# First attention pass with keys stationary, and a list scheduler that prices TensorE's tiling modes

## The chip, the cores and the metric

The kernel runs on one core of one Trainium2 chip. The time is device microseconds of one execution, from launch to the last store; runs of the kernel before took 632.1, 632.15 and 632.55 us (median 632.15). Profiles come from one execution that the hardware profiler recorded.

## What is computed

Two batches of eight heads, 1152 keys, head size 64. Queries are averaged in pairs, so each head has 576 of them. Then two dense layers follow on the 1152 rows that the attention gives.

```python
q_pool = q.reshape(B, H, S // 2, 2, D).mean(axis=3)
scores = scale * np.matmul(q_pool, k.transpose(0, 1, 3, 2))
scores = scores - np.max(scores, axis=-1, keepdims=True)
attn = np.exp(scores)
attn = attn / (np.sum(attn, axis=-1, keepdims=True) + 1e-09)
x = np.matmul(attn, v)                       # -> 1152 x 512
h = x @ w_in                                 # 512 -> 2048
g = np.maximum(h, 0.0) + np.log1p(np.exp(-np.abs(h)))
x = g @ w_out                                # 2048 -> 512
h = np.maximum(np.maximum(x @ w1, x @ w2), x @ w3)
out = h @ w_out2                             # 512 -> 768 -> 512
```

A common shift in place of each row's maximum gives the same softmax, as long as no exponential overflows and no sum gets too small; the kernel judges that at the end and would run a slow exact program if it failed.

## The kernel before

The heads are worked in eight pairs; the two heads of a pair lie on partitions 0 to 63 and 64 to 127, so that two matmuls with 64 contraction rows run side by side. Three arrangements of TensorE occur. In *row* matmuls (64*128 in the profile) the array is split by rows, one half for each head: the scores (`st`, tile by tile transposed, and `s`). In *column* matmuls (128*64) it is split by columns: values (`x`) and sums (`l`). *Whole-array* matmuls (128*128) are transposes of queries and keys (`tq`, `tk`), the spreading of the maximum (`tm`), the tail scores and all of the dense layers.

For each pair there are two passes. The first pass (`first_pass`, `scores`, `part_max`) finds a bound on the scores: a rough product of high halves, `s`, with queries stationary (128 at a time) and keys streaming in 384 columns; each result fills a PSUM bank, and VectorE reduces it to a maximum (L916). Four tiles of 128 queries make twelve row pairs. The last 64 queries of both heads stand together in a block-diagonal tile `qd` and make three whole-array matmuls (L904). `whole_max`, `spread` (L941) and `keep_shift` turn the maxima into a shift, one after six of nine row sets and one after all. The second pass (`one_unit`, `turned`, L956) computes the scores again, transposed and with three terms, in units of half a pair's queries (288 columns; three smaller units for pair 0): for each of nine key tiles a *block* `st` of six row matmuls into two banks, two exponentials on ScalarE (L966) that free the banks, an add into `acc` (L975, on GpSimd, one in each odd unit on VectorE), and for each three key tiles a group `x` (L983). `l` (L997) sums up.

PSUM has eight banks: two for `x`, six that `tq`, `tk`, `s`, `st`, `tm`, `l` and early weight conversion share. A bank is free again when the engine that reads it has finished.

The order of all this is made by `Order`, a list scheduler: every piece has an engine, a cost and a place; in a simulated timeline the piece with the lowest place among those that can start goes next. The first pass of pair n+1 is mixed into the second pass of pair n in this way. Weights of the first dense layer are converted with the lowest priority. Engines keep the order so found; each waits on semaphores.

Of the kernel before, what the change touches and what calls it, by code (L numbers as in the profile page):

```python
# [33 lines left out]
AK = {"load": -419.68, "load1": -714.981, "q1": -406.536, "k1": 649.535, "v0": 1846.393, "p1": 0.482, "p2": 18.929, "kl": 220.139, "c0": -292.838, "v": 170.415, "q": -14.042, "k": -7.013, "pass": 14.039, "gap": 4.467, "values": 59.704, "sum": 64.591}  # L34
WINDOW = 48.719
NPT = 20
ON_DVE = ((), (7,))
# [4 lines left out]
PAIR = 0.22  # L42
# [11 lines left out]
class Order:  # L54
# [3 lines left out]

    AFTER = {"PE": 0.30, "ACT": 0.22, "DVE": 0.20, "POOL": 0.22, "SP": 2.6, "AQ": 2.6}

    def __init__(self, **pools):
        self.work = []
        self.wrote = {}
        self.read = {}
        self.pools = pools
        self.got = {}
        self.ahead = {}

# [73 lines left out]
def kernel(  # L142
# [601 lines left out]
    else:  # L744
        order = Order(s=6)
        TRIO = 0.42
# [6 lines left out]
        NX = 2 * NT + 1  # L753
        ROWS = (0, 1, 2, NT, NT + 1, NT + 2, 3, NT + 3, 2 * NT)
        STEPS = ((0, 6), (6, NX))
        FIRST_ROWS = (0, NT, 1, 2, NT + 1, NT + 2, 3, NT + 3, 2 * NT)
        FIRST_STEPS = ((0, 2), (2, 6), (6, NX))
        KT = NJ // NB

# [3 lines left out]
        qds = []  # L763
        for n in range(2):
            qd = st.tile([P, P], F32R, tag=f"qd{n}", name=f"qd_{n}")
            nc.gpsimd.memset(qd.bitcast(F32), 0.0)
            qds.append(qd)
# [91 lines left out]
        def tail_q(pr, i, n):  # L859
            o = (NT - q_parts(pr)[1][0]) * QB  # L860
            nc.scalar.mul(qds[pr % 2][halves(i), halves(i)], tiles[n][halves(i), o : o + D], Q_SCALE)

# [36 lines left out]
        def scores(pr, t, g, *ns):  # L899
            qh, kh = tiles["qh", pr], tiles["kh", pr]  # L900
            cols = slice(g * BK, (g + 1) * BK)
# [10 lines left out]
        def part_max(pr, x, g, n):  # L912
            if ("nh", pr) not in tiles:
                tiles["nh", pr] = sm.tile([P, NX, NB], F32, tag=f"nh{pr % 2}", name=f"nh_{pr}")
            at = rows(pr).index(x)
            nc.vector.tensor_reduce(  # L916
                out=tiles["nh", pr][:, at, g : g + 1], in_=tiles[n][:, :BK], axis=AX.X, op=ALU.max, negate=True
            )
# [4 lines left out]
        def rows(pr):  # L923
            return ROWS if pr else FIRST_ROWS

        def rows_of(pr, step):
            return (STEPS if pr else FIRST_STEPS)[step]

        def whole_max(pr, step):
            if ("nm", pr) not in tiles:  # L930
                tiles["nm", pr] = sm.tile([P, 3], F32, tag=f"nm{pr % 2}", name=f"nm_{pr}")
                tiles["shift", pr] = sm.tile([P, 3], F32, tag=f"shift{pr % 2}", name=f"shift_{pr}")
            z = rows_of(pr, step)[1]
            nc.vector.tensor_reduce(
                out=tiles["nm", pr][:, step : step + 1], in_=tiles["nh", pr][:, :z], axis=AX.XY, op=ALU.min
            )
# [113 lines left out]
        def name_of(n):  # L1050
            return f"b{n[1]}"
# [6 lines left out]
        def prepare_first():  # L1058
# [4 lines left out]
            for g, (t0, t1) in enumerate(q_parts(0)):  # L1063
# [4 lines left out]
                if g:  # L1068
                    for i in range(2):
                        order.add("ACT", 0.16, p + 1, tail_q, 0, i, n, reads=(name_of(n),), writes=(f"qd0{i}",))  # L1070
# [8 lines left out]
        def prepare(pr):  # L1079
# [6 lines left out]
            for g in range(2):  # L1086
# [3 lines left out]
                if g:  # L1090
                    for i in range(2):
                        order.add("ACT", 0.16, p, tail_q, pr, i, n, reads=(name_of(n),), writes=(f"qd{y}{i}",))
# [7 lines left out]
        def first_pass(pr):  # L1100
            y = pr % 2
            gap = AK["gap"] if pr else 2.0
            k = 0
            for step, (a, z) in enumerate(STEPS if pr else FIRST_STEPS):
# [3 lines left out]
                some = rows(pr)[a:z]  # L1108
                for t in sorted({NT if x == 2 * NT else x % NT for x in some}):
                    xs = (2 * NT,) if t == NT else (t, NT + t)  # L1110
                    for g in range(NB):
                        p = at + gap * k
                        k += len(xs) / NB
                        ns = [next_bank() for _ in xs]
                        order.add("PE", PAIR if len(xs) == 2 else 0.18, p, scores, pr, t, g, *ns,
                                  reads=[f"kh{y}{g}", f"tq{y}", f"tk{y}"] + ([f"qd{y}0", f"qd{y}1"] if t == NT else [f"qh{y}{int(t >= (3 if pr else 1))}"]),
                                  writes=[name_of(n) for n in ns], take=tuple(ns))
                        for x, n in zip(xs, ns):
                            order.add("DVE", 0.49, p, part_max, pr, x, g, n, reads=(name_of(n),), writes=(f"nh{y}_{x}{g}",), free=n)
                p = at + gap * k  # L1120
                n = next_bank()
                order.add("DVE", 0.16, p - 2, whole_max, pr, step, reads=[f"nh{y}_{x}{g}" for x in some for g in range(NB)],
# [4 lines left out]
        def one_unit(u):  # L1127
# [3 lines left out]
            for j in range(NJ):  # L1131
# [3 lines left out]
                order.add("PE", TRIO * max(part, 0.8), p, turned, u, j, *ns,  # L1135
# [9 lines left out]
            for js in VALUES:  # L1145
                p = at + gap * js[-1] + AK["values"] * part
                order.add("PE", 0.48 * len(js) * part + 0.15, p, values, u, js,
                          reads=[f"p{(u * NJ + j) % NPT}" for j in js] + [f"v{y}"], writes=(f"x{u % 2}",))
            n, p = next_bank(), at + gap * NJ + AK["sum"] * part
            order.add("PE", (0.54 + 0.48 * len(DIRECT)) * part, p, sum_up, u, n,  # L1150
# [403 lines left out]
```

## Time and profile before

| | us |
|---|---|
| median of three runs | 632.15 |
| the profiled execution, by its own time | 632.11 |
| its span, first to last instruction | 630.3 |
| TensorE busy in the span | 607.8 |
| VectorE, ScalarE, GpSimd busy | 411.2, 355.6, 356.3 |
| last attention matmul ends and the first dense layer begins | 265.42 |

The attention fills the span up to 265.42 us, the dense layers the rest. In the profile a matmul in 32-bit floats (`x`, `l`, `tm`) shows as two records. A matmul's length in the timeline holds the way through the array, which the next one overlaps; how long a stretch of TensorE's work took is therefore read from one row's start to the next row's start. "Idle before" in brackets is the time in which nothing was in the array, and who ended it.

### The profile page before, as it was taken

The numbers are of one execution on the slowest core, as the hardware profiler recorded it, in microseconds if no ns is written. First come the engines' busy times: TensorE is split into PE (matmuls) and PEld (weight loads), VectorE is DVE, ScalarE is ACT, GpSimd is POOL, SyncE is SP. The second block draws the span as 40 slices with busy tenths as digits, with TensorE's granted clock in tenths as the row PEclk, the third lists the DMA queues.
The fourth block names the chain that finished last, engine by engine and source line by source line (L and its number), as shares of the span: only waits on it lengthen the run. The fifth ranks groups of instructions, "written<-read, shape, count | busy, mean of one in ns | idle before, by whom it ended". The sixth has DMA issues, their size and how long they took to land.

```text
span 630.3 us, 10804 instructions
## 1 busy us (share of the span) xinstructions
PE 607.8 (96%) x3992; PEld 510.6 (81%) x3992; DVE 411.2 (65%) x797; ACT 355.6 (56%) x833; POOL 356.3 (57%) x304
## 2 busy tenths in 40 slices
PE   6999999999999999999999999999999999999995
PEld 4766665666666565689999999999999999999994
DVE  6575757575758898688988897987879831121221
ACT  2557676766676777887767666775754312012101
POOL 1457676767678678399888787797865200000000
PEclk9999999999999999999999999999999999999999
DMA  6412131404051323123434243322323201000001
GB/s 156 145 39 77 38 92 23 109 6 116 33 143 35 106 68 101 35 68 105 124 108 125 82 128 101 108 93 68 100 80 123 68 1 51 0 2 35 17 1 56
DMA packets 53296, 46.68 MB, mean 74 GB/s; under 512 B 20592, under 2 KB 47216, under 8 KB 53232
## 3 DMA queue, kind: packets, MB, share of 16 engines
q1 hardware_dynamic: 51408, 45.29, 24.4%
q10 hardware_dynamic: 1824, 0.59, 0.4%
q8 instruction: 33, 0.54, 0.4%
q14 instruction: 31, 0.25, 0.1%
HBM read 43.52 MB, written 2.36 MB: 73 GB/s over the span
## 4 chain that ended last, share of the span: by engine, by line
PE 81%; ACT 6%; POOL 6%; issue 2%; DVE 2%; DMA 1%; ACTq 0%; SPq 0%; POOLq 0%
PE bank_h_m L1220 18%; PE bank_y L1220 15%; PE bank_h L1220 13%; PE x L983 10%; PE st L956 10%; PE bank_o L1220 6%; ACT p L966 4%; PE s L908 3%; POOL acc L975 2%; PE l L997 2%; PE tk L878 1%; POOL d L1275 1%; DVE nh L916 1%; PE tq L844 1%; PE s L904 1%
## 5 line engine op out<-in xcount | busy, mean ns | idle before, releaser
L966 ACT ACTIVATE p<-st,shift 128x288 f32<-128x288 f32 (+2 forms) x306 | 126.8, 487 | 65.8 <-PE st L956 58.9
L975 POOL TENSOR_TENSOR acc<-acc,p 128x576 f32<-128x576 f32 (+2 forms) x88 | 117.2, 1332 | 28.2 <-ACT p L966 24.2
L916 DVE TENSOR_REDUCE nh<-s 128x1 f32<-128x384 f32 x216 | 108.7, 550 | 32.1 <-PE s L908 27.3
L1220 PE MATMUL bank_h_m<-x,wh 128*128 128x384 f32 x432 | 114.1, 337 | 0.0
L1220 PE MATMUL bank_h<-x,wh 128*128 128x384 f32 x384 | 106.0, 338 | 0.7 <-DVE gl L1299 0.7
L241 POOL TENSOR_SCALAR size<-size 128x512 f32<-128x512 f32 x56 | 84.1, 1505 | 18.7 <-ACT size L236 18.7
L983 PE MATMUL x<-p,v 128*64 128x288 f32 (+2 forms) x612 | 81.5, 403 | 0.0
L1220 PEld LDWEIGHTS bank_h_m<-x,wh 128*128 128x128 f32 x432 | 78.8, 188 | 0.7
L956 PE MATMUL st<-qh,kh 64*128 64x288 f32 (+2 forms) x306 | 69.9, 358 | 6.3 <-ACT p L966 5.2
L1220 PE MATMUL bank_h_m<-x,wl 128*128 128x384 f32 x216 | 72.9, 337 | 0.0
L1220 PEld LDWEIGHTS bank_h<-x,wh 128*128 128x128 f32 x384 | 70.3, 188 | 1.4 <-DVE gl L1299 1.0
L956 PEld LDWEIGHTS st<-qh,kh 64*128 64x128 f32 x306 | 38.8, 192 | 39.4 <-ACT p L966 18.8
L1220 PE MATMUL bank_y<-gh,wh 128*128 128x384 f32 x192 | 65.2, 340 | 1.4 <-DVE gl L1299 1.4
L1220 PE MATMUL bank_y<-gl,wh 128*128 128x384 f32 x192 | 65.0, 339 | 0.0
L1220 PE MATMUL bank_y<-gh,wl 128*128 128x384 f32 x192 | 65.0, 339 | 0.0
L1220 PE MATMUL bank_h<-x,wl 128*128 128x384 f32 x192 | 64.9, 338 | 0.0
L1275 POOL TENSOR_TENSOR d<-e,d 128x384 f32<-128x384 f32 x48 | 49.0, 1020 | 25.7 <-DVE d L1268 23.9
L983 PEld LDWEIGHTS x<-p,v 128*64 128x64 f32 x612 | 39.7, 138 | 26.7 <-issue 8.2
L956 PE MATMUL st<-ql,kh 64*128 64x288 f32 (+2 forms) x306 | 56.7, 312 | 0.0
L956 PE MATMUL st<-qh,kl 64*128 64x288 f32 (+2 forms) x306 | 52.4, 297 | 0.0
L1284 POOL TENSOR_TENSOR d<-u,d 128x384 f32<-128x384 f32 x48 | 49.0, 1021 | 3.7
L1337 DVE TENSOR_TENSOR mg<-bank_h_m,mg 128x384 f32<-128x384 f32 x18 | 10.0, 555 | 61.5 <-PE bank_h_m L1220 61.5
(223 smaller groups left out, 1153.4 us busy)
## 6 DMA issues: line engine op xcount, KB each, us to landing
raw<-in_moe_w_out_dram SPq DMA_DIRECT2D x22, 512.0 KB, 3.6
raw<-in_moe_w_dram SPq DMA_DIRECT2D x18, 512.0 KB, 3.6
raw<-in_moe_w_in_dram SPq DMA_DIRECT2D x16, 512.0 KB, 3.8
v<-in_v_dram SPq DMA_DIRECT2D x16, 288.0 KB, 3.2
k<-in_k_dram SPq DMA_DIRECT2D x14, 288.0 KB, 4.8
q<-in_q_dram SPq DMA_DIRECT2D x14, 256.0 KB, 4.1
out_dram<-ob SPq DMA_DIRECT2D x9, 256.0 KB, 2.3
qm<-in_q_dram SPq DMA_DIRECT2D x15, 32.0 KB, 4.1
```

Of the source, the lines that this page charges most:

```text
L241: nc.gpsimd.tensor_scalar(out=size, in0=size, scalar1=SMALLEST, scalar2=None, op0=ALU.max)
L908: nc.tensor.matmul(tos[i][:, :BK], qh[halves(i), t * QB : (t + 1) * QB], kh[halves(i), cols], start=True, stop=True)
L916: nc.vector.tensor_reduce(out=tiles["nh", pr][:, at, g : g + 1], in_=tiles[n][:, :BK], axis=AX.X, op=ALU.max, negate=True)
L956: nc.tensor.matmul(tos[i], key[halves(i), cols], query[halves(i), some], start=term == 0, stop=term == len(terms) - 1)
L966: nc.scalar.activation(out=tiles["p", u, j][:, i, :W], in_=tiles[n][:, :W], func=AF.Exp, bias=shift)
L975: engine.tensor_tensor(out=acc, in0=first, in1=tiles["p", u, j][:, :, :W], op=ALU.add)
L983: nc.tensor.matmul(x[halves(i), :W], tiles["v", pr][:, i, j], tiles["p", u, j][:, i, :W], start=(j == 0), stop=(j == NJ - 1),)
L997: nc.tensor.matmul(tiles[n][halves(i), :W], ones, part[:, i, :W], start=part is parts[0], stop=part is parts[-1])
L1220: nc.tensor.matmul(ps, lhs(a, kk), rhs(bb, kk), start=start and n == 0, stop=stop and n == last)
L1275: nc.gpsimd.tensor_tensor(out=d, in0=gs["e", i], in1=d, op=ALU.subtract)
L1284: nc.gpsimd.tensor_tensor(out=d, in0=gs["u", i], in1=d, op=ALU.add)
L1337: nc.vector.tensor_tensor(out=to, in0=hp, in1=g, op=ALU.max)
```

## The change

The first pass swaps its operands: 128 keys are stationary, and the queries stream. For pairs 1 to 7 there are two steps: nine key tiles with 512 query columns, one bank for each head and tile, and nine with the last 64 columns, five or four key tiles side by side in a bank. For pair 0 the steps are the three units' own columns (128, 224, 224), three or two key tiles in a bank. `qd`, its memsets, its two ScalarE copies and the three whole-array matmuls go. The maxima are kept by step; in pair 0 each step's shift comes from that step alone. `spread` makes two 64-column matmuls in place of one of 128. `Order` knows for each TensorE piece its mode (rows, columns, whole), adds a cost where the mode changes, and prefers, by `stay`, a piece of the mode it is in. The table of places is another; units of pair 0 may run in another order, and the add of key tile 7 on VectorE goes to GpSimd.

```diff
-ON_DVE = ((), (7,))
+ON_DVE = ((), (8,))
 DIRECT = (8,)
-PAIR = 0.22
+    CHANGE = {"rows": 0.21, "columns": 0.11, "whole": 0.15}
...
+        mode = [self.mode.get(w[3].__name__, "whole") if w[0] == "PE" else None for w in work]
+        last = {}
...
-                _, n = min((place, n) for s, place, n in can if s <= t)
+                _, n = min((place + (self.stay if mode[n] != last.get(e) else 0.0), n) for s, place, n in can if s <= t)
...
+            if mode[n] != last.get(e):
+                cost += self.CHANGE[mode[n]]
+                last[e] = mode[n]
...
+        order.mode = dict.fromkeys(("scores", "turned"), "rows") | dict.fromkeys(("values", "sum_up", "spread"), "columns")
+        order.stay = AK["stay"]
...
+        def steps(pr):
+            if pr:
+                return [(0, BANK, [(j,) for j in range(NJ)]), (BANK, NQ - BANK, [range(5), range(5, NJ)])]
+            out = [(0, P, [range(g * KT, (g + 1) * KT) for g in range(NB)])]
+            return out + [(c0, W, [range(j, min(j + 2, NJ)) for j in range(0, NJ, 2)]) for _, c0, W in UNIT[1:3]]
...
-            if t == NT:
-                to = bank(ns[0], f"s_{pr}_{2 * NT}_{g}")
-                nc.tensor.matmul(to[:, :BK], qds[pr % 2], kh[:, cols], start=True, stop=True)
-                return
-            tos = [bank(n, f"s_{pr}_{i * NT + t}_{g}") for i, n in enumerate(ns)]
-            for i in range(2):
-                nc.tensor.matmul(
-                    tos[i][:, :BK], qh[halves(i), t * QB : (t + 1) * QB], kh[halves(i), cols], start=True, stop=True
-                )
+            c0, W, some = steps(pr)[step]
+            tos = [bank(n, f"s_{pr}_{step}_{x}_{i}") for i, n in enumerate(ns)]
+            for o, j in enumerate(some[x]):
+                for i in range(2):
+                    nc.tensor.matmul(
+                        tos[i][:, o * W : (o + 1) * W],
+                        kh[halves(i), j * P : (j + 1) * P],
+                        qh[halves(i), c0 : c0 + W],
+                        start=True,
+                        stop=True,
+                    )
...
-            nm = tiles["nm", pr][:, step : step + 1].to_broadcast([P, P])
-            nc.tensor.matmul(to[:, :P], nm, ident, start=True, stop=True)
+            nm = tiles["nm", pr][:, step : step + 1].to_broadcast([P, D])
+            for i in range(2):
+                nc.tensor.matmul(to[halves(i), :P], nm, ident, start=True, stop=True)
```

On TensorE in the middle of the attention, between two groups of values, the kernel before has this (first number in a name: the pair for `s` and `tm`, the unit for `st`, `l` and `x`):

```order
L956 MATMUL st_9_1_1_2142<-qh_4_1668,kl_4_1690 128x288
L941 MATMUL tm_4_1_2151<-ident_94,nm_4_2026 128x128
L904 MATMUL s_5_8_0_2154<-kh_5_2110,qd_1_104 128x384
L904 MATMUL s_5_8_1_2158<-kh_5_2110,qd_1_104 128x384
L904 MATMUL s_5_8_2_2161<-kh_5_2110,qd_1_104 128x384
L997 MATMUL l_8_2166<-acc_8_1937,ones_106 64x288
```

and the changed kernel this at the same place:

```order
L881 MATMUL tk_5_2_2124<-ident_94,k_5_1885 128x128 x3
L983 MATMUL x_8_1979<-p_8_3_1987,v_3_1394 64x288 x2
L983 MATMUL x_8_1979<-p_8_4_2008,v_3_1394 64x288 x2
L983 MATMUL x_8_1979<-p_8_5_2021,v_3_1394 64x288 x2
L941 MATMUL tm_4_1_2149<-ident_94,nm_4_2048 64x128 x2
L956 MATMUL st_9_1_0_2153<-qh_4_1696,kh_4_1709 128x288
```

The tail's three whole-array matmuls are gone, and `tm`, now a column matmul, has moved next to a group of values.

A little later, where first-pass and second-pass scores alternate, the kernel before has on TensorE

```order
L908 MATMUL s_5_0_0_2238<-kh_5_2110,qh_5_2089 128x384
L908 MATMUL s_5_4_0_2239<-kh_5_2110,qh_5_2089 128x384
L956 MATMUL st_9_6_0_2247<-qh_4_1668,kh_4_1689 128x288
L956 MATMUL st_9_6_1_2248<-qh_4_1668,kh_4_1689 128x288
L956 MATMUL st_9_6_0_2247<-ql_4_1669,kh_4_1689 128x288
L956 MATMUL st_9_6_1_2248<-ql_4_1669,kh_4_1689 128x288
L956 MATMUL st_9_6_0_2247<-qh_4_1668,kl_4_1690 128x288
L956 MATMUL st_9_6_1_2248<-qh_4_1668,kl_4_1690 128x288
L908 MATMUL s_5_0_1_2257<-kh_5_2110,qh_5_2089 128x384
L908 MATMUL s_5_4_1_2258<-kh_5_2110,qh_5_2089 128x384
L983 MATMUL x_9_2213<-p_9_3_2210,v_4_1716 64x288 x2
```

(the end of a run of four, `st s st s`), and the changed kernel

```order
L956 MATMUL st_9_3_1_2198<-qh_4_1696,kl_4_1710 128x288
L908 MATMUL s_5_0_1_0_2206<-qh_5_2116,kh_5_2129 128x512
L908 MATMUL s_5_0_1_1_2207<-qh_5_2116,kh_5_2129 128x512
L956 MATMUL st_9_4_0_2212<-qh_4_1696,kh_4_1709 128x288
L956 MATMUL st_9_4_1_2213<-qh_4_1696,kh_4_1709 128x288
L956 MATMUL st_9_4_0_2212<-ql_4_1697,kh_4_1709 128x288
L956 MATMUL st_9_4_1_2213<-ql_4_1697,kh_4_1709 128x288
L956 MATMUL st_9_4_0_2212<-qh_4_1696,kl_4_1710 128x288
L956 MATMUL st_9_4_1_2213<-qh_4_1696,kl_4_1710 128x288
L983 MATMUL x_9_2222<-p_9_0_2110,v_4_1814 64x288 x2
```

(the end of a run of three, `st s st`). One 512-column pair stands where two of 384 stood, and the run between two value groups holds three bank pairs.

At the start, around the first shift of pair 0, TensorE had

```order
L904 MATMUL s_0_8_0_198<-kh_0_139,qd_0_102 128x384
L904 MATMUL s_0_8_1_209<-kh_0_139,qd_0_102 128x384
L941 MATMUL tm_0_0_213<-ident_94,nm_0_206 128x128
L904 MATMUL s_0_8_2_216<-kh_0_139,qd_0_102 128x384
L956 MATMUL st_0_0_0_220<-qh_0_131,kh_0_139 128x128
```

and now has

```order
L908 MATMUL s_0_2_2_0_217<-qh_0_131,kh_0_135 128x224
L908 MATMUL s_0_2_2_1_218<-qh_0_131,kh_0_135 128x224
L941 MATMUL tm_0_0_225<-ident_94,nm_0_214 64x128 x2
L956 MATMUL st_0_0_0_230<-qh_0_131,kh_0_135 128x128
L956 MATMUL st_0_0_1_231<-qh_0_131,kh_0_135 128x128
```

Scores of pair 0's last columns take the tail's place; the shift itself stands where it stood.

## Rows read from the trace of the kernel before

**Rows 1.** By stage: stretch, length, busy PE, PEld, DVE, ACT, POOL, clock, DMA share, GB/s.

```profile
123.55:153.75 30.20, 29.05 (x242) 18.55 (x241) 19.49 (x43) 20.80 (x55) 20.98 (x17) 1.00 0.21 54
183.98:216.62 32.64, 30.93 (x242) 19.26 (x242) 26.28 (x55) 24.54 (x64) 24.59 (x18) 1.00 0.31 85
216.62:265.42 48.80, 46.45 (x392) 29.38 (x391) 40.83 (x75) 38.37 (x94) 35.39 (x25) 1.00 0.25 76
265.42:293.18 27.76, 25.70 (x147) 25.05 (x145) 22.25 (x44) 22.87 (x50) 24.78 (x23) 1.00 0.24 77
```

**Rows 2.** TensorE's timeline in one pair's window: start, length, engine, line, what.

```profile
125.16 0.40 PE L956 MATMUL st<-qh,kh 64*128 64x288 f32 x2
...
126.47 0.40 PE L956 MATMUL st<-qh,kh 64*128 64x288 f32 x1 [0.35 <-ACT p L966]
...
127.23 1.68 PE L983 MATMUL x<-p,v 128*64 128x288 f32 x12
128.84 0.40 PE L956 MATMUL st<-qh,kh 64*128 64x288 f32 x2
...
129.20 0.29 PE L956 MATMUL st<-qh,kl 64*128 64x288 f32 x2
129.33 0.34 PE L908 MATMUL s<-kh,qh 64*128 64x384 f32 x2
...
131.68 1.68 PE L983 MATMUL x<-p,v 128*64 128x288 f32 x12
133.29 0.40 PE L956 MATMUL st<-qh,kh 64*128 64x288 f32 x2
...
134.05 0.71 PE L997 MATMUL l<-acc,ones 128*64 128x288 f32 x4
...
149.90 0.90 PE L904 MATMUL s<-kh,qd 128*128 128x384 f32 x3
150.73 0.71 PE L997 MATMUL l<-acc,ones 128*64 128x288 f32 x4
```

**Rows 3.** TensorE's timeline, two later runs of three blocks and what follows them.

```profile
195.92 0.40 PE L956 MATMUL st<-qh,kh 64*128 64x288 f32 x2
...
198.22 0.46 PE L983 MATMUL x<-p,v 128*64 128x288 f32 x2
...
258.97 0.40 PE L956 MATMUL st<-qh,kh 64*128 64x288 f32 x2
...
260.37 0.71 PE L997 MATMUL l<-acc,ones 128*64 128x288 f32 x4
```

**Rows 4.** Groups of one window by shape, VectorE and GpSimd: count, busy, mean ns.

```profile
L916 DVE TENSOR_REDUCE nh<-s 128x1 f32<-128x384 f32 x28 | 14.1, 551 | 5.3 <-PE s L908 3.3 <-PE s L904 1.8
L975 POOL TENSOR_TENSOR acc<-acc,p 128x576 f32<-128x576 f32 x12 | 17.0, 1413 | 3.3 <-ACT p L966 2.7
```

**Rows 5.** TensorE's timeline, the first 34 us.

```profile
13.64 0.57 PE L956 MATMUL st<-qh,kh 64*128 64x128 f32 x2
...
23.56 1.11 PE L844 MATMUL tq<-ident,qs 128*128 128x128 f32 x4
...
26.63 0.67 PE L904 MATMUL s<-kh,qd 128*128 128x384 f32 x1
27.23 0.55 PE L956 MATMUL st<-qh,kh 64*128 64x224 f32 x2
...
28.77 1.01 PE L904 MATMUL s<-kh,qd 128*128 128x384 f32 x2
29.71 1.45 PE L983 MATMUL x<-p,v 128*64 128x128 f32 x12
...
31.98 0.88 PE L983 MATMUL x<-p,v 128*64 128x128 f32 x12
...
32.99 0.28 PE L956 MATMUL st<-ql,kh 64*128 64x224 f32 x2
33.10 0.28 PE L956 MATMUL st<-qh,kl 64*128 64x224 f32 x2
```

More of the change, by code (lines that the diff above doesn't have):

```diff
@@ L32 @@
 BANK = 512
-AK = {"load": -419.68, "load1": -714.981, "q1": -406.536, "k1": 649.535, "v0": 1846.393, "p1": 0.482, "p2": 18.929, "kl": 220.139, "c0": -292.838, "v": 170.415, "q": -14.042, "k": -7.013, "pass": 14.039, "gap": 4.467, "values": 59.704, "sum": 64.591}
-WINDOW = 48.719
+AK = {"load": 18.806, "load1": -361.956, "q1": 465.624, "k1": -601.474, "v0": -174.412, "p1": 16.097, "p2": -1.542, "kl": 95.048, "c0": -340.25, "v": 83.029, "q": -26.274, "k": -25.681, "pass": 2.655, "gap": 2.142, "values": 111.836, "sum": 55.437, "stay": 33.792}
+WINDOW = 25.652
 NPT = 20
-ON_DVE = ((), (7,))
+ON_DVE = ((), (8,))
 VALUES = ((0, 1, 2), (3, 4, 5), (6, 7, 8))
@@ L67, in __init__ @@
         self.ahead = {}
+        self.mode = {}
+        self.stay = 0.0
     def add(self, engine, cost, place, f, *args, reads=(), writes=(), take=None, free=None):
@@ L752 @@
         UNITS = len(UNIT)
[L753 to L757, printed above, removed]
+        def steps(pr):
[3 more added lines that the diff above has]
+            return out + [(c0, W, [range(j, min(j + 2, NJ)) for j in range(0, NJ, 2)]) for _, c0, W in UNIT[1:3]]
         KT = NJ // NB
+        NX = 26
         def halves(i):
             return slice(i * D, (i + 1) * D)
[L763 to L767, printed above, removed]
         ones = home.tile([P, D], F32, tag="ones", name="ones")
@@ L897, in low_k, with scores, part_max @@
             )
-        def scores(pr, t, g, *ns):
+        def scores(pr, step, x, *ns):
             qh, kh = tiles["qh", pr], tiles["kh", pr]
-            cols = slice(g * BK, (g + 1) * BK)
-            if t == NT:
-                to = bank(ns[0], f"s_{pr}_{2 * NT}_{g}")
-                nc.tensor.matmul(to[:, :BK], qds[pr % 2], kh[:, cols], start=True, stop=True)
-                return
-            tos = [bank(n, f"s_{pr}_{i * NT + t}_{g}") for i, n in enumerate(ns)]
-            for i in range(2):
-                nc.tensor.matmul(
-                    tos[i][:, :BK], qh[halves(i), t * QB : (t + 1) * QB], kh[halves(i), cols], start=True, stop=True
-                )
-        def part_max(pr, x, g, n):
+            c0, W, some = steps(pr)[step]
[9 more added lines that the diff above has]
+                    )
+        def part_max(pr, step, x, i, n):
             if ("nh", pr) not in tiles:
-                tiles["nh", pr] = sm.tile([P, NX, NB], F32, tag=f"nh{pr % 2}", name=f"nh_{pr}")
-            at = rows(pr).index(x)
+                tiles["nh", pr] = sm.tile([P, NX], F32, tag=f"nh{pr % 2}", name=f"nh_{pr}")
+            _, W, some = steps(pr)[step]
+            at = 2 * (sum(len(steps(pr)[a][2]) for a in range(step)) + x) + i
             nc.vector.tensor_reduce(
-                out=tiles["nh", pr][:, at, g : g + 1], in_=tiles[n][:, :BK], axis=AX.X, op=ALU.max, negate=True
+                out=tiles["nh", pr][:, at : at + 1], in_=tiles[n][:, : W * len(some[x])], axis=AX.X, op=ALU.max, negate=True
             )
@@ L921, in step_of @@
             return [w for w in range(UNITS) if UNIT[w][0] == UNIT[u][0]].index(u)
[L923 to L927, printed above, removed]
         def whole_max(pr, step):
@@ L932, in whole_max @@
                 tiles["shift", pr] = sm.tile([P, 3], F32, tag=f"shift{pr % 2}", name=f"shift_{pr}")
-            z = rows_of(pr, step)[1]
+            a, z = (2 * sum(len(some) for _, _, some in steps(pr)[:n]) for n in (0 if pr else step, step + 1))
             nc.vector.tensor_reduce(
-                out=tiles["nm", pr][:, step : step + 1], in_=tiles["nh", pr][:, :z], axis=AX.XY, op=ALU.min
+                out=tiles["nm", pr][:, step : step + 1], in_=tiles["nh", pr][:, a:z], axis=AX.X, op=ALU.min
             )
@@ L1067, in prepare_first @@
                 order.add("ACT", (0.21, 0.5)[g], p, high_q, 0, g, n, reads=(name_of(n),), writes=(f"qh0{g}",) if g else ("qh00", "qh01"))
-                if g:
-                    for i in range(2):
-                        order.add("ACT", 0.16, p + 1, tail_q, 0, i, n, reads=(name_of(n),), writes=(f"qd0{i}",))
                 order.add("DVE", (0.22, 0.55)[g], AK["c0"], low_q, 0, g, n, reads=(name_of(n), f"qh0{g}"), writes=(f"ql0{g}",), free=n)
@@ L1101, in first_pass @@
             y = pr % 2
-            gap = AK["gap"] if pr else 2.0
+            gap = AK["gap"] if pr else 1.0
             k = 0
-            for step, (a, z) in enumerate(STEPS if pr else FIRST_STEPS):
+            for step, (c0, W, some) in enumerate(steps(pr)):
                 at = WINDOW * (pr - 1) + AK["pass"] if pr else (-50.0, AK["p1"], AK["p2"])[step]
@@ L1107, in first_pass @@
                     k = 0
[L1108 to L1119, printed above, removed]
+                parts = [g for g in range(2) if c0 < q_cols(pr, g).stop and c0 + W > q_cols(pr, g).start]
+                for x, js in enumerate(some):
+                    p = at + gap * k
+                    k += 1
+                    ns = [next_bank() for _ in range(2)]
+                    order.add("PE", max(0.107, W * 0.00046) * len(js), p, scores, pr, step, x, *ns,
+                              reads=sorted({f"kh{y}{j // KT}" for j in js}) + [f"tq{y}", f"tk{y}"] + [f"qh{y}{g}" for g in parts],
+                              writes=[name_of(n) for n in ns], take=tuple(ns))
+                    for i, n in enumerate(ns):
+                        order.add("DVE", 0.083 + len(js) * W / 960, p, part_max, pr, step, x, i, n, reads=(name_of(n),),
+                                  writes=(f"nh{y}_{step}{x}{i}",), free=n)
                 p = at + gap * k
                 n = next_bank()
-                order.add("DVE", 0.16, p - 2, whole_max, pr, step, reads=[f"nh{y}_{x}{g}" for x in some for g in range(NB)],
+                order.add("DVE", 0.16, p - 2, whole_max, pr, step, reads=[f"nh{y}_{b}{x}{i}" for b in range(0 if pr else step, step + 1) for x in range(len(steps(pr)[b][2])) for i in range(2)],
                           writes=(f"nm{y}_{step}",))
@@ L1134, in one_unit @@
                 parts = range(1 if pr == 0 and step_of(u) == 0 else 2)
-                order.add("PE", TRIO * max(part, 0.8), p, turned, u, j, *ns,
+                order.add("PE", TRIO * max(part, 0.78), p, turned, u, j, *ns,
                           reads=[f"tq{y}", f"tk{y}"] + [f"{x}{y}{g}" for x in ("qh", "ql") for g in parts] + [f"{x}{y}{j // KT}" for x in ("kh", "kl")] + [f"nm{y}_{step_of(u)}"],
@@ L1146, in one_unit @@
                 p = at + gap * js[-1] + AK["values"] * part
-                order.add("PE", 0.48 * len(js) * part + 0.15, p, values, u, js,
+                order.add("PE", 0.475 * len(js) * part, p, values, u, js,
                           reads=[f"p{(u * NJ + j) % NPT}" for j in js] + [f"v{y}"], writes=(f"x{u % 2}",))
             n, p = next_bank(), at + gap * NJ + AK["sum"] * part
-            order.add("PE", (0.54 + 0.48 * len(DIRECT)) * part, p, sum_up, u, n,
+            order.add("PE", (0.475 + 0.475 * len(DIRECT)) * part, p, sum_up, u, n,
                       reads=[f"acc{u % 2}"] + [f"p{(u * NJ + j) % NPT}" for j in DIRECT], writes=(name_of(n),), take=n)
```

8 lines of the change are left out of this document (1 added, 7 removed).

## The prediction

> **What bounds the kernel.** I read the page first, then the busy time by stage, then TensorE's timeline of a window, then the groups by shape. The stages show TensorE busy in nearly all of every stretch while the other engines stand at two thirds: in a pair's window of 30.20 us TensorE has 29.05, VectorE 19.49, ScalarE 20.80, GpSimd 20.98 [rows 1]. So TensorE's own queue sets the time, in the attention (to 265.42) and after it. The dense layers are not touched; what can change is where the attention ends and how far the other engines lag there.
>
> The busy time hides a second thing. In the timeline the starts of rows tell what a piece really takes. A pair of 288-column row matmuls goes in 0.13 (129.20 to 129.33), a block `st` of three such pairs in 0.40, a value group in 1.61 (127.23 to 128.84) [rows 2]. Now take the *runs* of row matmuls between two column groups. Blocks `st` and pairs `s` (0.17, scaled from 0.13 by columns) fill two banks each, and six banks are shared. A run of two (133.29 to 134.05) takes 0.76, 0.19 over its streaming of 0.57: the price of going into rows and out again. A run of four (125.16 to 127.23) takes 2.07 for 1.14, 0.93 over, and in its midst TensorE stands 0.35 because a ScalarE exponential has not freed a bank. A run of six (128.84 to 131.68) takes 2.84 for 1.71, 1.13 over [rows 2]. A run of three is between: 0.21 over (258.97 to 260.37, streaming 1.19) where ScalarE is free, 1.34 over (195.92 to 198.22, streaming 0.96) where early weight conversion takes a bank and VectorE's time [rows 3]. In a window of 30.20 the eight runs (two each of two, three, four and six) stand about 5.7 over their streaming; one visit per run, 0.2, cannot go, so about 4 are stalls by bank.
>
> By TensorE's busy time a window could lose at most 30.20 − 29.05 = 1.15; by the starts, about 4. The Trainium skill ("Trainium Kernel Development and Optimization", Performance Expectations) says that matmul busy time is a bad metric of the distance to the roofline, because matmuls are pipelined. By that rule the 1.15 is no ceiling, and the trace agrees: weight loads are busy for 18.55 of the same 30.20 [rows 1].
>
> **The change, part by part, in a middle window.** Streaming: out go twelve 384-column pairs (12 × 0.17 = 2.1) and the tail, 0.83 with its way out (149.90 to 150.73) [rows 2]. In come nine 512-column pairs, 0.23 each by scaling = 2.1, and nine pairs of 64 columns. No row shows these. Pairs of 224 columns go in 0.11 (32.99 to 33.10) [rows 5] where 288 take 0.13; scaling would give 0.10, so a floor is near. Between 0.03 (by columns) and 0.11 I take 0.11: nine are 1.0, at least 0.3. Net +0.1. `tm` in two column halves does the same streaming, and one of the two now joins a value group: −0.1. Visits: three whole-array visits become one; row and column visits are one more each. About nothing in sum.
>
> Against this stands a rule of the Trainium skill ("TensorEngine Tiling (Array Packing)", When to Use Tiling): with at most 64 streaming columns swap stationary and streaming operand. That is what the old tail did. By it the swap back costs the 1.0 − 0.83 = 0.17 a window, little over 1 us in seven pairs; it is in the sum.
>
> Stalls: in the order of the changed kernel a middle window has nine runs: five of three, two of two, one of four, one of six. The three-runs are `st s st` between value groups. After the last `st` the value group gives ScalarE and VectorE 1.6 us; four exponentials and two reductions of up to 0.551 × 512/384 = 0.735 [rows 4] fit in it, so I charge 0.25, near the row at 258.97. Sum 5 × 0.25 + 2 × 0.2 + 0.93 + 1.13 = 3.7, against 5.7: −2.0. A middle window goes from 30.2 to 28.3.
>
> By stage, each from the order's runs priced like this:
> - Start to the first value group (29.71 [rows 5]). Before the first `st` (13.64) the pace is set by loads, reductions and the shift, which stand where they stood: 0. Behind it four 384-column pairs go (0.35 each at half the clock: 1.4), pair 1's query transposes (1.1), the tail's matmuls of pair 1 (0.6 and 0.94 by the starts 26.63, 27.23, 28.77, 29.71) and three whole-array visits (about 0.3 each at this pace: 0.9); five 224-column pairs come in (0.21 each: 1.0). Sum −4.0.
> - First value group to that of unit 3: that work arrives here, with three runs of five: +1.9.
> - Unit 3 to 5: seven whole-array visits become one, the rest as above: −3.6. Unit 5 to 7: two runs of four and one of five: −1.3. Units 7 to 11: two middle windows, −3.8.
> - Unit 11 to 13, 32.64, and 13 to the end, 48.80 [rows 1]: runs are no shorter than before, and three-runs cost about 1 here: −0.7.
>
> Sum −11.5 at the attention's end. At the hand-over TensorE waits 27.76 − 25.70 = 2.06 [rows 1] while GpSimd has 24.78 of work in 27.76. GpSimd takes over eight adds, 8 × 1.41 = 11.3 [rows 4], one a window, and arrives more loaded; the new order puts a sixth dense product ahead of the second product's. I give back 1.0 (0 to 4). Total −10.5. Against the profiled execution's 632.11 (the runs' median is 632.15) that is **621.6**.
>
> Costed at nothing: the five fewer reductions a window (the same columns, VectorE has 10 us free), the two query copies less on ScalarE (free for 9), the memsets, and the loads of v for units 0 and 1, which trade places on SP's queue so that the earlier group's come first. If the spare time of VectorE goes, banks come late, which is the slower rival. The first shift of a later pair adds a tighter wait: its `tm` stands in TensorE's queue behind three blocks and five 64-column pairs that follow the last 512-column pair (3 × 0.40 + 5 × 0.11 = 1.75), in which two reductions of at most 0.735 and a small one must end. That just fits; if it does not, `tm` holds four 64-column pairs and the blocks behind it. I take 0, and keep 0.5 a window.
>
> **The clock.** Until about 31 us TensorE runs at 1.2 GHz: the same group of 128-column values has 1.45 at 29.71 and 0.88 at 31.98 [rows 5]. The rise came after 224-column row pairs (27.23) and the first value group had started; these move some 4 us earlier. If the rise comes with them, the start's gain stands, if it stays at 31, half of 4 is lost: ±2.
>
> **Rivals.**
> 1. *Banks come late everywhere, slower.* A 512-column reduction holds its bank up to 0.18 longer than 0.551, and GpSimd's extra adds hold `l`. From the first value group on there are 26 three-runs. If each cost what the row at 195.92 shows (1.34) in place of 0.25, they would lose 28; at 0.95 each, 18, and the time is 632.1 − 10.5 + 18 = 640. It decides from 0.65 a run on, where the gain is eaten. For it: the 1.34, and VectorE 26.28 of 32.64 there. Against it: 19.49 of 30.20 in middle windows.
> 2. *Only the start gains.* Stalls move but do not shrink; the new runs of five and six cost what the old fours did. 632.1 − 4.0 + 1.9 − 1 = 629. For it: streaming and visits are equal by the sum above, so all rests on run lengths.
> 3. *Stalls shrink further.* If pieces now start when their banks are free, the 21 runs of four and more cost 0.65 in place of about 1.05: 8 less, 613. For it: a run of five at 1.1 is a loss of ScalarE's phase, which a better order can avoid.
> 4. *TensorE's busy time is the ceiling* (1.15 a window over seven, with the start's 4.0 − 1.9): −9, within the forecast's own range.
>
> **Chances.** Forecast 0.55 (own range 617 to 627), rival 1 0.13, rival 2 0.14, rival 3 0.18. Leaving out the far parts of 1 and 3 gives 612 to 634. 0.2% is 1.3 us, about what can be told from no change here. Faster: 0.55 + 0.18 + 0.10 of rival 2 = 0.83; same 0.05; slower 0.12.
>
> **What would show it.** Right: middle windows of about 28.3, three-runs about 1.2 to 1.3 long, first value group near 25.7, clock up before 30, 64-column pairs at 0.11. Wrong: idle before `st` ended by VectorE's reductions (rival 1); windows still at 30 (rival 2); pairs of 64 columns slower than 0.11; a first dense product that waits, or more than 4 us of TensorE idle behind it.

## The result, and the profile after

The changed kernel takes 618.11 us (median of four runs, 617.12 to 618.81) against 632.35 for the kernel before (four runs, among them the three whose median was 632.15): a ratio of 0.9773 (95% interval 0.9756 to 0.979). Forecast were 621.6, so the gain is 14.2 where 10.5 were expected. Times of kernels here and below are medians; of e6's four runs the one at a lower granted clock (669.78 us, 0.966 where the others have 0.98) is left out. The profiled execution took 618.21, its span 616.4. The first dense matmul, which marks the attention's end in this document, starts at 252.94 in place of 265.42. TensorE is busy for 600.3 us (607.8 before), GpSimd for 366.8 (356.3).

By stage, after (columns as in [rows 1]): two middle windows, units 11 to 13, from there to the attention's end, and the first dense product.

```profile
116.92:145.00 28.08, 27.84 (x256) 18.45 (x254) 18.90 (x38) 20.19 (x53) 22.36 (x18) 1.00 0.26 64
145.00:173.33 28.33, 27.99 (x257) 18.39 (x255) 18.97 (x38) 21.30 (x55) 22.36 (x18) 1.00 0.35 99
173.33:203.97 30.64, 29.79 (x259) 19.25 (x257) 28.12 (x54) 23.69 (x61) 26.52 (x20) 1.00 0.41 113
203.97:252.94 48.97, 46.81 (x409) 29.69 (x409) 37.36 (x66) 39.75 (x102) 37.77 (x27) 1.00 0.20 64
252.94:281.00 28.06, 27.21 (x153) 26.55 (x154) 24.82 (x44) 20.80 (x45) 25.63 (x25) 1.00 0.26 81
```

A middle window (units 7 to 9, 9 to 11) is 2.1 and 1.9 shorter than the 30.20 of [rows 1]; GpSimd has 1.4 more in it, the add that moved.

TensorE's timeline after, in the first of these windows:

```profile
131.99 0.40 PE L956 MATMUL st<-qh,kh 64*128 64x288 f32 x2
...
132.71 0.72 PE L956 MATMUL st<-qh,kh 64*128 64x288 f32 x2
133.06 0.50 PE L956 MATMUL st<-ql,kh 64*128 64x288 f32 x2
...
134.06 0.93 PE L908 MATMUL s<-qh,kh 64*128 64x64 f32 x10
...
135.39 0.44 PE L941 MATMUL tm<-ident,nm 128*64 128x128 f32 x4
135.76 0.63 PE L908 MATMUL s<-qh,kh 64*128 64x64 f32 x8
136.23 0.38 PE L956 MATMUL st<-qh,kh 64*128 64x288 f32 x2
...
143.78 0.40 PE L956 MATMUL st<-qh,kh 64*128 64x288 f32 x2
...
144.28 0.39 PE L908 MATMUL s<-qh,kh 64*128 64x512 f32 x2
144.51 0.30 PE L956 MATMUL st<-qh,kh 64*128 64x288 f32 x2
...
145.00 0.46 PE L983 MATMUL x<-p,v 128*64 128x288 f32 x2
```

Pieces of a run are blocks `st`, 512-column pairs `s` and groups of 64-column pairs; a three-run has three of them. The three-run at the end takes 1.22 (143.78 to 145.00), 0.20 over its streaming of 1.02. The 512-column pair goes in 0.23 (144.28 to 144.51), four 64-column pairs in 0.47 (135.76 to 136.23), 0.117 each. The run of six at 131.99 takes 3.40 for 2.35. Its second `st` needs 0.35 for its first pair (132.71 to 133.06) where 0.13 is usual: the wait stands inside the row, which gets longer (0.72), and is not listed as idle time.

Adding up every run of row matmuls from 31 us on by its starts, the time over streaming falls from 46.6 us in 72 runs to 36.1 in 68. Whole-array visits fall from 29 to 7 (6.9 to 2.6 us), column visits cost 1.9 more. Together that is 12.9, about the 12.5 by which the first dense matmul starts earlier. Of the 1.9, however, 1.35 is no column work. Behind the last value group TensorE stands idle until VectorE's L1022 has freed the bank of `l`:

```profile
249.91 1.68 PE L983 MATMUL x<-p,v 128*64 128x288 f32 x12
...
252.94 0.41 PE L1213 MATMUL bank_h<-x,wh 128*128 128x384 f32 x1 [1.35 <-DVE rr L1022]
```

The kernel before has no wait there. Its last attention matmul ends at 265.49 and the changed kernel's at 251.59, so the attention's own matmuls are done 13.9 earlier. The start's own gain (3.6) is nearly taken back by unit 3 (60.48, before 61.50), where work of the start arrives.

### The profile page after: what moved, and what is told of

Its sections match the earlier page's. It is cut to its first block, busy times and chain, and to the rows that moved or that the text cites. A ratio compares the mean times of both kernels' runs of the same rounds, so it can differ in the third digit from the quotient of the medians.

```text
span 616.4 us, 10975 instructions
## 1 busy us (share of the span) xinstructions
PE 600.3 (97%) x4116; PEld 512.3 (83%) x4116; DVE 407.1 (66%) x753; ACT 349.6 (57%) x817; POOL 366.8 (60%) x310
## 4 chain that ended last, share of the span: by engine, by line
PE 89%; DVE 5%; ACT 2%; POOL 1%; issue 1%; DMA 1%; SPq 0%; ACTq 0%; DVEq 0%; POOLq 0%
PE bank_h_m L1213 18%; PE bank_y L1213 16%; PE bank_h L1213 14%; PE st L956 12%; PE x L983 11%; PE bank_o L1213 6%; PE s L908 5%; PE l L997 2%; PE tk L881 2%; DVE nh L921 1%; ACT p L966 1%; DMA k<-in_k_dram 1%; PE tm L941 1%; PE tq L851 1%; DVE t L259 1%
## 5 line engine op out<-in xcount | busy, mean ns | idle before, releaser
L975 POOL TENSOR_TENSOR acc<-acc,p 128x576 f32<-128x576 f32 (+2 forms) x96 | 128.2, 1335 | 15.6 <-ACT p L966 9.0
L921 DVE TENSOR_REDUCE nh<-s 128x1 f32<-128x512 f32 (+5 forms) x180 | 105.5, 631 | 40.5 <-PE s L908 40.0
L956 PE MATMUL st<-qh,kh 64*128 64x288 f32 (+2 forms) x306 | 65.4, 351 | 1.7 <-DVE nh L921 1.0
L956 PE MATMUL st<-ql,kh 64*128 64x288 f32 (+2 forms) x306 | 54.5, 308 | 0.0
L908 PE MATMUL s<-qh,kh 64*128 64x512 f32 (+3 forms) x306 | 51.1, 368 | 0.7 <-DVE nh L921 0.3
```

The source lines that it names most:

```text
L908: nc.tensor.matmul(tos[i][:, o * W : (o + 1) * W], kh[halves(i), j * P : (j + 1) * P], qh[halves(i), c0 : c0 + W], start=True, stop=True,)
L921: nc.vector.tensor_reduce(out=tiles["nh", pr][:, at : at + 1], in_=tiles[n][:, : W * len(some[x])], axis=AX.X, op=ALU.max, negate=True)
L956: nc.tensor.matmul(tos[i], key[halves(i), cols], query[halves(i), some], start=term == 0, stop=term == len(terms) - 1)
L975: engine.tensor_tensor(out=acc, in0=first, in1=tiles["p", u, j][:, :, :W], op=ALU.add)
```

## Experiments

Theory: the gain is in the order, in which fewer pieces come to a bank that is not free. Rivals: the swapped operands themselves, the scheduler's knowledge of modes, VectorE's reductions. The table puts all runs side by side; "attention's end" is the start of the first dense matmul, "over" is the time of row runs over their streaming from 31 us on, "window" the time from unit 7 to unit 9, all from row starts. Averages by run length below are taken from 60 us on.

| kernel | us | attention's end | over | window |
|---|---|---|---|---|
| before | 632.35 | 265.42 | 46.6 | 30.20 |
| changed | 618.11 | 252.94 | 36.1 | 28.08 |
| e1 modes, old first pass | 635.57 | 268.29 | 44.6 | 31.78 |
| e2 new first pass, no modes | 633.23 | 267.72 | 46.8 | 30.28 |
| e3 half reductions | 617.40 | 251.72 | 34.9 | 27.80 |
| e4 half exponentials too | (below) | 249.83 | 31.7 | 27.27 |
| e5 no `stay` | 626.93 | 260.55 | 41.6 | 29.25 |
| e6 five banks | 661.43 | 295.78 | 74.3 | 32.40 |
| e7 whole `tm` | 620.17 | 255.36 | 36.1 | 28.36 |
| e8 64-column pairs twice | 625.44 | 261.78 | 36.3 | 29.08 |
| e9 add 7 on VectorE | 629.25 | 261.61 | 42.8 | 29.04 |
| e10 places a | 611.92 | 246.62 | 30.2 | 27.40 |
| e11 places b | 617.83 | 251.74 | 31.5 | 28.08 |
| e12 places c | 609.80 | 245.16 | 30.3 | 27.44 |

TensorE's granted clock is 1.00 in every window of the last column. Elsewhere in the attention some of these profiles have stretches at 0.50, the lower of its two levels (1.2 GHz in place of 2.4): one of some 3.4 in e1 (from 203.10), e2 (203.60) and e9 (210.55), two in e8 (81.55, 112.25), and 40.65 to 54.35 and 238.65 to 245.50 in e6. Before these two of e6 TensorE had stood waiting (busy for 2.05 of the 2.60 from 38.00 to 40.60, 1.23 of the 2.60 from 236.00 to 238.60). At most half of such a stretch is lost, as an estimate from the two levels: 1.7 of the 3.4, 10 of e6's 20.6.

**Where the gain comes from: e1, e2, e5.**

```diff
# e1: the kernel before, with mode costs and order.stay = 0.0
+    CHANGE = {"rows": 0.21, "columns": 0.11, "whole": 0.15}
# e2: the changed kernel
-    CHANGE = {"rows": 0.21, "columns": 0.11, "whole": 0.15}
+    CHANGE = {"rows": 0.0, "columns": 0.0, "whole": 0.0}
# e2 and e5
-        order.stay = AK["stay"]
+        order.stay = 0.0
```

> The kernel before with its old first pass (queries stationary, block-diagonal tail) and its old table of places, but the scheduler adds the three mode costs (0.21, 0.11, 0.15); stay is 0. Theory (the gain comes from the order: shorter row runs and better spread pieces): priced by its row runs (33 of three or fewer more than before, whole-array visits 33) it stands 2.1 under the kernel before, so about 630 us. Rival A (the scheduler's knowledge of the modes is the gain by itself): about 621. Rival B (the swap of operands is the gain): 632, no change.

> The changed kernel with the new first pass and the new table, but the scheduler's mode costs and stay are all 0, as in the kernel before. The same instructions in another order: 14 whole-array visits after the first value group in place of 7, 76 column visits in place of 70, three-runs 15 in place of 26, runs of four and more 25 in place of 21. Theory (order): priced by runs 6.6 over the changed kernel, about 625 us. Rival B (the swap itself is the gain, whatever the order): within 1.5 of 618.

> The changed kernel with the scheduler's mode costs kept and the preference for the current mode (stay) set to 0. Another order of the same instructions: whole-array visits 15 in place of 7, three-runs 17 in place of 26, runs of four and more 22 in place of 21. Priced by row runs it stands 5.2 over the changed kernel (623); the run with the mode costs at 0 as well came out 9 above such a price, so theory (order, run lengths): 623 to 631. Rival (the mode costs alone make the order; stay adds little): 618 to 620.

e2 has the changed kernel's instructions in another order, and the whole gain is gone: ratio to before 1.0005 (0.9996 to 1.0015). In this order the swap by itself brings nothing. e1 is slower than before, 1.0049 (1.0032 to 1.0066): knowing the modes brings nothing either where the table was not made for it. Its expected 630 and e2's 625 were misses, because a price by run length alone (four-runs 0.95) held neither there (1.30 on average) nor in e2 (runs of six 1.44). e5 gives back 8.8 of the 14.2. So with the new instructions it is the order, made by table, mode costs and `stay` together, that earns the gain. Whether the old first pass would do as well with a table found for it was not tried; that rival is open.

The window of e2, columns as in [rows 1]:

```profile
123.56:153.84 30.28, 29.57 (x256) 18.46 (x255) 18.75 (x38) 20.59 (x53) 22.39 (x17) 1.00 0.23 56
```

The same 256 matmul records stand in it as in the changed kernel's 28.08, and the other engines have the same work to 0.4 us.

**Who holds the banks: e3, e4, e6.**

```diff
# e3, e4 (512-column reductions read 256)
-                in_=tiles[n][:, : W * len(some[x])], ...
+                in_=tiles[n][:, : 256 if W == BANK else W * len(some[x])], ...
# e4
+            Z = W if u < 5 else W // 2
+            if Z < W:
+                nc.vector.memset(tiles["p", u, j][:, i, Z:W], 0.0)
-            nc.scalar.activation(out=...[:, i, :W], in_=tiles[n][:, :W], func=AF.Exp, bias=shift)
+            nc.scalar.activation(out=...[:, i, :Z], in_=tiles[n][:, :Z], func=AF.Exp, bias=shift)
# e6
-        order = Order(s=6)
+        order = Order(s=5)
```

> The changed kernel, order unchanged, but each 512-column reduction of the first pass reads 256 columns (the maxima leave out half of those queries). VectorE then frees 63 pairs of banks about 0.27 us earlier. Theory: what is left over streaming in row runs is mostly ScalarE's rate (two exponentials of a block take about 0.9 us, its matmuls 0.40), only the 1.0 us of idle that the trace puts down to reductions goes: 615.5 to 618. Rival (banks held by VectorE set the runs of three and more): 0.2 for each of 47 such runs, about 609.

> As the run with halved reductions, and from unit 5 on each exponential reads and writes 144 of 288 columns (the rest of p is set to zero by VectorE, so the attention is not computed fully). TensorE's instructions and order are unchanged. Theory: row runs are held up by banks that ScalarE has not yet freed; with 0.6 us for two exponentials in place of 0.9 the runs of four and more fall from about 0.95 to 1.2 over their streaming to about 0.4: 604 to 611 us. Rival (the time over streaming belongs to the row matmuls themselves, their weight loads and mode changes): within 1.5 of the run with halved reductions.

> The changed kernel with five banks in place of six for tq, tk, s, st, tm and l; the scheduler knows it and orders anew (three-runs 19 in place of 26, runs of five and more 19 in place of 12). Theory (the cost of a run comes from the number of bank pairs: up to three pieces start at once, the fourth waits until the first piece's exponentials have freed its banks; with five banks the third waits): every run of three and more costs some 0.4 to 0.6 more, 45 runs, so 18 to 27 on top: 636 to 645. Rival (cost by run length alone, whatever the banks): 3.4 over the changed kernel, 621.5.

e3: 0.7 less, as the theory had it, and no more than the two kernels' runs scatter; the length of the reductions is not what holds the runs. e4's sums make the kernel's own judgement run the slow exact program behind the attention (1252.24 us in all), so only its attention is read: from unit 5 to the end 160.5, against 163.3 in e3. That is 2.8 less where some 5 to 13 were expected. In the window of the table the run of six falls from the changed kernel's 1.06 over to 0.67, the four-run from 0.78 to 0.62, not to 0.4. The exponential shrank less than its columns, from 502 to 378 ns; VectorE's added memsets may hide a part, and how much of the rest is the way from TensorE to ScalarE and back is not separated.

e6 shows the banks at work, far more than expected (661.4, not 636 to 645). The scheduler made a new order for it, and a part of the 43 belongs to the half clock, 10 at most. But a window at full clock takes 32.40, 4.3 more than the changed kernel's, and three-runs go from 0.31 over on average to about 1.1. TensorE's timeline of one, `s st st`:

```profile
168.53 0.50 PE L908 MATMUL s<-qh,kh 64*128 64x512 f32 x2
168.87 0.43 PE L956 MATMUL st<-qh,kh 64*128 64x288 f32 x2
...
169.14 0.42 PE L956 MATMUL st<-qh,kl 64*128 64x288 f32 x2
169.81 0.83 PE L956 MATMUL st<-qh,kh 64*128 64x288 f32 x2 [0.25 <-DVE nh L921]
170.25 0.52 PE L956 MATMUL st<-ql,kh 64*128 64x288 f32 x2
...
170.84 0.46 PE L983 MATMUL x<-p,v 128*64 128x288 f32 x2
```

The third piece starts 0.67 after the last pair of the second (169.14), when the reduction of the first has freed a bank. With six banks a three-run costs 0.31 over on average and a four-run 0.93: mostly it is the fourth piece that waits, though not always (the third one does at 132.71 above).

**What the new pieces cost: e7, e8.**

```diff
# e7
-            for i in range(2):
-                nc.tensor.matmul(to[halves(i), :P], nm, ident, start=True, stop=True)
+            nc.tensor.matmul(to[:, :P], nm, ident, start=True, stop=True)   # nm broadcast to [P, P]
# e8
-                for i in range(2):
+                for i in (0, 1, 0, 1) if W == NQ - BANK else range(2):
```

> The changed kernel, order unchanged, but the spread of the maximum is one whole-array matmul of 128 columns again in place of two of 64. By the trace of the kernel before a whole-array tm between rows takes 0.42 from start to start; of 17 in the changed kernel 9 stand beside a value or sum group, where they add 0.22, and 5 in the middle stand alone at 0.37. Theory: 9 x 0.2 + 5 x 0.05 and the start's three, +2.0 to 2.5: 620 to 620.6. By the scheduler's own mode costs: +3.8, 622. Rival (the split is worth nothing): 618.

> The changed kernel, order unchanged, but each 64-column matmul of the first pass is issued twice: 63 more pairs, same result. If such a pair costs 0.11 wherever it stands: +7, 625. Theory: in the runs of five and six these pairs go while a block waits for its banks, so there a part is absorbed (5 pairs a window); the four behind tm are not: +3 to +6, 621 to 624. If pairs stream by their columns (0.03): +2, 620.

e7 costs 2.1, as priced from the rows. In e8 a window with nine more 64-column pairs is 1.00 longer (29.08), 0.11 a pair, and nothing of it is absorbed in the long runs: that part of the theory fell. (The stretches from unit 3 to 5 and from 5 to 7, which hold e8's two stretches at half clock, are 2.5 longer each, some 1.5 of it the clock's.)

**An add in VectorE's queue: e9.**

```diff
-ON_DVE = ((), (8,))
+ON_DVE = ((), (7,))
```

> The changed kernel with the add of key tile 7 in odd units back on VectorE (ON_DVE as in the kernel before); eight adds less on GpSimd, and the scheduler makes an order around it: three-runs 30 in place of 26, runs of four and more 19 in place of 21. If run lengths alone set the time: 0.3 less, 617.8. If the forecast's term was right (GpSimd arrives loaded at the hand-over and that costs 1.0): 617. Theory with banks: VectorE's queue then holds a 1 us add ahead of the reductions that free banks, in windows where it has spare time but is awaited: estimated by replaying the engines' orders with the durations and latencies of the six traces so far (which gives their attention within 1.4 us): +7, 625.

11.1 slower, where 7 were expected. The scheduler made a new order around the add, so add and order are not told apart. By stage, the middle windows lose 0.7 to 1.0 each, though VectorE has only 19.3 of work in the 29.04 and GpSimd is relieved: about the add's own 0.75. Most of the loss, 6.2, stands from unit 11 to the last attention matmul, where VectorE is busy for 30.88 of 33.16 up to unit 13, and where the half clock takes at most 1.7. What those 6.2 consist of was not taken apart. VectorE's and TensorE's timelines of e9, and then of the changed kernel at the same place (a sum's inverse, with a run `s st st` begun):

```profile
125.64 0.47 DVE L1020 SCALAR_TENSOR_TENSOR l<-l,rr 128x288 f32<-128x288 f32 x1 [0.59 <-ACT rr L1014]
...
126.02 0.75 DVE L975 TENSOR_TENSOR acc<-acc,p 128x576 f32<-128x576 f32 x1
...
126.39 0.29 PE L956 MATMUL st<-qh,kh 64*128 64x288 f32 x1
...
126.68 1.28 DVE L921 TENSOR_REDUCE nh<-s 128x1 f32<-128x512 f32 x2
127.20 0.40 PE L956 MATMUL st<-qh,kh 64*128 64x288 f32 x1 [0.52 <-ACT p L966]
...
127.88 0.45 DVE L1022 SCALAR_TENSOR_TENSOR rr<-l,rr 128x288 f32<-128x288 f32 x1
```

```profile
123.44 0.47 DVE L1020 SCALAR_TENSOR_TENSOR l<-l,rr 128x288 f32<-128x288 f32 x1 [0.59 <-ACT rr L1014]
...
123.94 0.46 DVE L1022 SCALAR_TENSOR_TENSOR rr<-l,rr 128x288 f32<-128x288 f32 x1
...
124.31 2.50 DVE L921 TENSOR_REDUCE nh<-s 128x1 f32<-128x512 f32 x4
```

L1022 frees the bank of `l`. In the changed kernel it ends at 124.40, right behind L1020. In e9 the add and two reductions stand between, the bank stays taken until 128.33, and the second half of the third piece starts 0.81 after the first (126.39, 127.20), when an exponential has freed another bank. This three-run takes 1.12 over; there is one like it in each middle window, the others stay at 0.20 to 0.34. With one bank gone, it has e6's illness.

**Other tables: e10, e11, e12.** The instructions of the changed kernel, other numbers in the table, and an offset for single pieces that is the same in all pairs. They were looked for with the engines' orders replayed by the durations and waits of the traces above.

```diff
-WINDOW = 25.652
+WINDOW = 24.266                            # e12; AK, CHANGE, TRIO, AFTER have other values too
+NUDGE = {('l', 0): -0.29, ('l', 1): 4.25, ('s', 0, 0): 0.21, ('s', 0, 1): -1.5, ...}
-                p, m = at + gap * j, u * NJ + j
+                p, m = at + gap * j + NUDGE.get(("st", u % 2, j), 0.0), u * NJ + j
```

> The changed kernel's instructions with another table of places, mode costs and latencies, and a small offset of its own for each key tile, value group, sum and first-pass piece of a pair (the same in every pair). Runs of four 2 in place of 9, but eight of five, three of six and four of eight. Replayed with the durations and latencies of the traces the attention ends 7.6 earlier; GpSimd is then some 5 later behind it than TensorE: 610.5 to 616. Rival (length of the runs alone counts): 2.3 less, 616. Rival (the changed kernel's order can't be bettered this way, the replay misses what matters): 618 to 625.

> As the run before with a third table, in which GpSimd is not behind at the attention's end. Replayed: the attention ends 6.2 earlier, so 612. By run lengths alone: 1.7 less, 616.4. Rival as there: 618 to 625.

> As the two runs with other tables of places, now with 28 pieces on TensorE before the first value group (34 in the run that took 611.9, 30 in the changed kernel) and the first three value groups close together, so that less work falls into the stretch in which rows run at half the clock. In the run at 611.9 the first value group came at 28.17 and rows were still slow at 31.41, and the first group of unit 3 at 62.93, 2.4 behind the changed kernel's 60.48. Theory (half the clock at the start costs what stands there): first value group near 25.5, unit 3 near 61, and with the middle windows at 27.4 to 27.8 a time of 609 to 612. Rival (the order before the first value group makes no difference, the middle alone counts): 612 to 614.

e12 is the fastest: 609.8, as expected, ratio to before 0.964 (0.9623 to 0.9656), below the changed kernel's interval. Its long run, of eight pieces, on TensorE (its lines stand one further down in the file):

```profile
130.09 0.40 PE L957 MATMUL st<-qh,kh 64*128 64x288 f32 x2
...
130.59 0.29 PE L957 MATMUL st<-qh,kh 64*128 64x288 f32 x2
...
131.00 0.82 PE L909 MATMUL s<-qh,kh 64*128 64x64 f32 x10
131.55 0.59 PE L957 MATMUL st<-qh,kh 64*128 64x288 f32 x2
...
132.13 0.80 PE L909 MATMUL s<-qh,kh 64*128 64x64 f32 x8
132.66 0.48 PE L957 MATMUL st<-qh,kh 64*128 64x288 f32 x2
...
134.28 0.33 PE L882 MATMUL tk<-ident,k 128*128 128x128 f32 x1
```

4.19 for a streaming of 3.34, 0.85 over for eight pieces, less than the changed kernel's 1.06 for six: the 64-column pairs stand after the second and the third block, 0.55 and 0.53 of work for TensorE, and could cover the time in which ScalarE frees banks. No run shows that this is the reason, and in e8 doubled pairs were not absorbed. In e10 the middle is as good, but the first value group comes at 28.17 and unit 3 at 62.93; in e12 at 24.17 and 61.14 (forecast 25.5 and 61). So e12 is 1.8 ahead by unit 3, of the 2.1 between the medians. e11 misses its 612: its first value group comes at 27.45 and unit 3 at 65.09, its window takes 28.08, and its dense part 364.7 where e12's takes 363.7.

## Why the prediction was right, and where it was not

By its steps, forecast against measured (row starts):

- Start to the first value group: −4.0; −3.6 (26.10, [rows 5] 29.71). The clock came with it: a 128-column value group has 1.34 at 26.10 and 0.88 at 28.34, where it had 1.45 at 29.71 and 0.88 at 31.98.

```profile
26.10 1.34 PE L983 MATMUL x<-p,v 128*64 128x128 f32 x12
...
28.34 0.88 PE L983 MATMUL x<-p,v 128*64 128x128 f32 x12
```

- To unit 3: +1.9; +2.6. Unit 3 to 5: −3.6; −3.7. Unit 5 to 7: −1.3; −1.9. Units 7 to 11: −3.8; −4.0. These steps stood.
- Units 11 to 13 and on to the last attention matmul: −0.7; −3.2. Mis-sized: three-runs were charged about 1 there and cost 0.19 to 1.23, 0.5 on average. Units 11 to 13 went from 32.64 to 30.64, with more VectorE work in it (28.12) than before, and 13 to the last matmul is 1.2 shorter.
- The hand-over: +1.0; 0.0. This step failed. The forecast put its wait down to GpSimd, which does arrive with 25.63 of work in 28.06, as charged. But from the end of the last attention matmul to the end of the span the kernel before needs 364.8 (630.3 − 265.49), the changed kernel 364.8 (616.4 − 251.59), and e9, with eight adds less on GpSimd, 364.8 as well (626.5 − 261.7). GpSimd's adds set nothing there. What TensorE waits for is VectorE: `gl`, with 2.1 in the kernel before and 2.0 in e9, and in the changed kernel L1022 ahead of the first dense matmul and less of `gl` behind it, 2.3 together. (Counted from the first dense matmul the rest looks 1.4 shorter, 363.5 after 364.9, because that wait stands ahead of the mark.) The changed kernel's waits from 252 us on (engine, line, releaser: us in total, times, longest):

```profile
PE bank_h L1213 <- DVE rr L1022: 1.4, 1, 1.4
PE bank_h L1213 <- DVE gl L1292: 0.6, 1, 0.6
PE bank_y L1213 <- DVE gl L1292: 0.3, 1, 0.3
```

- Three-runs were charged 0.25 and cost 0.31 on average (median 0.22). 64-column pairs: 0.11, measured 0.117 and by e8 0.11. The first shift's `tm` follows without idle time, so the tighter wait does fit.
- "Three-runs cost 0.25, fours 0.93, sixes 1.13" is a good sum for this kernel and no law: one three-run in each middle window of e9 costs 1.12, the runs of eight in e12's middle windows 0.85. By e6, what is priced is a piece that comes while all banks are held; run length stands for it only while the order around stays alike. How much of a long run's price is banks was not settled, as e4 took off 0.4 of 1.06.

The two steps that missed, units 11 to the last matmul and the hand-over, are 3.5 together, about the 3.4 by which the profiled execution (13.9 quicker) beat the forecast.

Of the rivals, the first (banks late everywhere) did not come, but e6 shows its mechanism and size: with one bank less a window at full clock takes 4.3 more. The second is out: by unit 3 only 1.0 of the 12.5 is there. The third (stalls shrink further, 613) did not come either: the 21 runs of four and more cost 1.07 on average, as forecast, not 0.65. e12 goes past its 613, with fewer such runs (17 from 31 us on, 0.9 each). The fourth, TensorE's busy time as a ceiling, falls: a window lost 2.1, not 1.15, and in e12 2.76. So the Trainium skill's sentence on matmul busy time ("Trainium Kernel Development and Optimization", Performance Expectations) is borne out by this trace. Its rule on at most 64 streaming columns ("TensorEngine Tiling (Array Packing)", When to Use Tiling) holds in direction: nine such pairs cost 1.0 a window where the old tail cost 0.83. The page joins column tiling to the swap; the old tail used the whole array, and no run shows the page's own form. The 0.17 is little beside the order.

## What to carry to other kernels

Where several engines share PSUM banks, count the banks that are free when each piece comes up, not the busy time of the engine that holds them: in e9 a new order with one add of 0.75 in front of the instruction that frees a bank cost 0.7 to 1.0 in every middle window, on an engine that is idle for a third of it. A change that brings both new instructions and a new order is taken apart by giving the new instructions an untuned order and looking whether anything is left. That shows what they bring in such an order, and not what the old instructions would do in a tuned one. When an order is searched, try short pieces that need few banks in the gap in which a long run waits, as e12 has them; that it was these that helped was not shown. Where a stage's wait can move across the mark that ends the stage, count from the last work of the stage before, or a wait looks like a gain.

## What was not expected of the hardware

A row matmul that waits for a bank is often no idle time in the profile: its row grows (0.72 for 0.40 at 132.71, where the second matmul of the pair starts 0.35 behind the first), and only the distance of starts shows the wait. Row pairs at the full clock did not get shorter than 0.11 us: 224 columns take 0.11 ([rows 5]), 64 take 0.11 to 0.117.
